# Other start addresses for the operands of the second MLP's matmuls, in a transform followed by two MLPs

## The chip, the cores and the metric

The kernel runs on one core of a Trainium2 chip, as one launch. The metric is the time of one execution in microseconds of device time; the kernel before takes 1510.42 us in the median of three runs (1510.21 to 1510.7). TensorE has two clock levels here, 1.2 and 2.4 GHz; the profile gives the granted clock as a share of the higher one.

## The reference

The input `x` has 4 batches of 3072 tokens with 256 features. A two-dimensional Fourier transform is taken over tokens and features and its real part kept. The result goes through an MLP and then through a second, gated one with a shift by one token:

```
x  = fft(fft(x, axis=1), axis=2).real                  # 12288 tokens, 256 features
h  = x @ w_in;  g = max(0.01 * h, h);  x = g @ w_out   # 256 -> 2048 -> 256
xk = mu_k * x + (1 - mu_k) * x_prev                    # x_prev: the token before
xr = mu_r * x + (1 - mu_r) * x_prev
k  = max(xk @ w_k, 0)                                  # 256 -> 1024
v  = (k * k) @ w_v                                     # 1024 -> 256
out = v / (1 + exp(-(xr @ w_r)))                       # gate, 256 -> 256
```

The weights come as 64-bit floats and are turned on the chip into pairs of 32-bit values.

## The kernel before

Precision is kept by pairs: each operand of a large matmul is held as a high and a low part in the type float32r, and a product is the sum of three matmuls, high by high, low weights by high, high weights by low. All large matmuls have 128 rows, 128 columns of weights and 512 moving columns. Moving and weight operands lie in SBUF; results go to PSUM.

The program has three stages in order of time. A set-up of some 120 us makes tables and the first weights. Then the transform and the first MLP run batch by batch in tiles of 512 tokens (until about 915 us). Last comes the second MLP in 24 tiles of 512 tokens (`for ti in range(len(tiles))`), which is the part that the change touches.

A tile of the second MLP is worked off in eight steps `f`, one for each 128 of the 1024 hidden features. In each step TensorE gets:

- six matmuls of `k_mm` (PSUM tile `kps`): the weights `kh`, `kl`, `kh` (called `wkh` and `wkl` in rows) against the mixed tokens `mh`, `mh`, `ml`, for two halves of the features each;
- in two of the eight steps six matmuls of `r_mm` (PSUM tile `rps`): `rh`, `rl`, `rh` against the high and low mix for the gate;
- six matmuls of `v_mm` (PSUM tile `v`) for a step that came two earlier: `vh`, `vl`, `vh` against the squared features `k2h`, `k2h`, `k2l`.

ScalarE and VectorE make in the meantime relu and square of a step (`k_ev`), its split in two parts (`k_split`) and the mix and split of the next tile (`prep`, one piece after each step). The lists `q1` and `q2` keep the squared features two steps ahead of `v_mm`. SP loads token tiles two ahead (`load_tile`) and stores results (`finish`). The engines follow this order as it is written; nothing reorders it.

Where a tile lies in SBUF is decided by pools: a pool puts the tags of its tiles one after the other in the order in which each tag is first asked for, a tag with several buffers taking several places. The six weights of the second MLP are the first tiles of the pool `w2p`, at the right end of SBUF, in the order kh, kl, vh, vl, rh, rl; everything else of this stage is in the pool `p2`. One small tile, `pad3`, begins `p2`. With it each of the six weight tiles and each tile of `p2` starts at 480 modulo 512 bytes of its partition. Slices within a tile start whole multiples of 512 bytes further on, so every moving operand and every weight block of these matmuls starts at 480 as well. There are two exceptions, both in the first tile of tokens: its mix (`prep_early`) and its first squared features lie in tiles of another pool, at 128 modulo 512. In the first MLP weights and moving operands start at 416, also alike.

Of the kernel before, what the change touches and what calls it, by code (L numbers as in the profile page):

```python
# [9 lines left out]
F32 = mybir.dt.float32  # L10
# [7 lines left out]
P = 128  # L18
# [29 lines left out]
def source(n):  # L48
    if n == 0:
        return D_, MID  # L50
    return (S_, place(n)) if n <= M else (D_, place(N - n))


def tile_tokens():
    at = {source(n): n for n in range(N)}
    return [[at[s, t * W + c] for c in range(W)] for s in (S_, D_) for t in range(NT)]


TOKENS = tile_tokens()


def runs_before(tokens):
    runs = []
    for c, n in enumerate(tokens):
        s, q = source(n - 1) if n else (None, 0)
        if runs and runs[-1][0] == s and s is not None and runs[-1][1] + runs[-1][3] == q:
            runs[-1][3] += 1
        else:
            runs.append([s, q, c, 1])
    return runs  # L70


def token_rows():
    rows = np.concatenate([np.array(t) for t in TOKENS])
    return np.concatenate([rows + b * N for b in range(B)])
# [3 lines left out]
def fft_mlp_kernel(ctx, tc, xa, xb, x7, x8, x87, tb, tbs, alt, ce, so, mu, w_in, w_out, w_k, w_v, w_r, out):  # L79
# [23 lines left out]
    def act_copy(o, i):  # L103
        A.activation(o, i, ACTF.Copy)  # L104
# [4 lines left out]
    def hi_lo(hi, lo, src):  # L109
        act_copy(hi, src)  # L110
        V.tensor_tensor(lo, src, hi.bitcast(F32), op=ALU.subtract)  # L111
# [556 lines left out]
    def w2_alloc():  # L668
        w2p = tc.alloc_tile_pool(name="w2p", bufs=1, side="right")
        w2["pool"] = w2p  # L670
        for nm, k, f in (("k", 2, FK), ("v", NK, D), ("r", 2, D)):
            for x in "hl":
                w2[nm + x] = w2p.tile([P, k, f], F32R, name=f"w{nm}{x}")
        w2["xp"] = tc.alloc_tile_pool(name="xp", bufs=1, side="right")
        for n in range(n_early):
            nm, _, at = sources[n]
            for x, k in zip("hl", kept[n]):
                Q.dma_start(at(w2[nm + x]).bitcast(F32), k)


    def w2_piece(n):
        z = {"fp": stage, "ft": "f"}
        nm, src, at = sources[n]

        def load():
            z["st"] = load_f64(src, 2, 256)

        def parts():
            if n < n_early:
                return (stage.tile([P, 2, 256], F32R, tag="r", bufs=3, name="wh"),  # L690
                        stage.tile([P, 2, 256], F32R, tag="h", bufs=2, name="wl"))
            return at(w2[nm + "h"]), at(w2[nm + "l"])

        one, two, three, four, five = split_steps(z, 2, 256, parts)

        def last():
            five()
            if n < n_early:
                for k, t in zip(kept[n], z["p"]):
                    Q.dma_start(k, t.bitcast(F32))  # L700
            if n + 1 < len(sources):
                w2_load[n + 1]()
        return load, [one, two, three, four, last]

    w2_load, w2_steps = [], []
    for n in range(len(sources)):
        a, c = w2_piece(n)
# [5 lines left out]
    def load_tile(ti):  # L713
# [5 lines left out]
        Q.dma_start(x, yd[b][s][:, :, t * W:(t + 1) * W])  # L719
        for s, q, c, n in runs_before(TOKENS[i]):  # L720
            if s is None:
# [5 lines left out]
    def prep(x, xprev, r):  # L727
        def mix(i, h, t, m):
            s = slice(2 * i + h, 2 * i + h + 1)
            A.activation(t[:, h], xprev[:, h], ACTF.Copy, scale=omu[:, s])  # L730
            V.scalar_tensor_tensor(m[:, h], x[:, h], mut[:, s], t[:, h], op0=ALU.mult, op1=ALU.add)

        def one(i, nm):
            z = {}

            def first():
                z["t"] = w2["p2"].tile([P, 2, W], F32, tag="mt", name="mt")
                z["m"] = w2["p2"].tile([P, 2, W], F32, tag="mx", name="mx")
                mix(i, 0, z["t"], z["m"])

            def split():
                hi = w2["p2"].tile([P, 2, W], F32R, tag=nm + "h", name="mh")
                lo = w2["p2"].tile([P, 2, W], F32R, tag=nm + "l", name="ml")
                hi_lo(hi, lo, z["m"])
                r[nm] = (hi, lo)
            return [first, lambda: mix(i, 1, z["t"], z["m"]), split]

        return one(0, "k") + one(1, "r")
# [34 lines left out]
    for b in range(B):  # L783
# [4 lines left out]
        for ti in range(NT):  # L788
# [3 lines left out]
            for u in range(NF):  # L792
                i = ti * NF + u
                x = nx
# [37 lines left out]
                if b == B - 1 and i == qe_u + 2:  # L832
                    fft.release()
                    w2_alloc()
# [79 lines left out]
    p2 = w2["p2"] = ctx.enter_context(tc.tile_pool(name="p2", bufs=2))  # L914
# [24 lines left out]
    def finish(ti, vps, sig):  # L939
# [5 lines left out]
        if ti < len(tiles) - 1:  # L945
            Q.dma_start(out[ti], o)

    def k_split(k2):
        hi = p2.tile([P, W], F32R, tag="k2h", bufs=3, name="k2h")
        lo = p2.tile([P, W], F32R, tag="k2l", bufs=3, name="k2l")  # L950
        hi_lo(hi, lo, k2)
        return hi, lo

# [13 lines left out]
    for ti in range(len(tiles)):  # L967
# [7 lines left out]
        for f in range(f0, NK):  # L975
            ps = ps2.tile([P, 512], F32, tag="k", bufs=2, name="kps")
            r = p2.tile([P, W], F32, tag="r", bufs=3, name="rl")
            k2 = p2.tile([P, W], F32, tag="k2", bufs=3, name="k2")
            k_mm(ps, f, rd["k"])
            k_ev(ps, r, k2)  # L980
            if q1:
                tt, ff, kk2 = q1.pop(0)
                q2.append((tt, ff, k_split(kk2)))
            q1.append((t, f, k2))
            t["rk"] = rd.get("r")
            if not end and g0 <= f < g0 + NB:
                gate(t, f - g0)
            if end and f == NK - 1:
                gate(t, 0)
            if len(q2) > 1:  # L990
                drain()
            if f == f0:
                for n in ((1, 2) if ti == 0 else (ti + 2,)):
                    if n < len(tiles):
                        loaded[n] = load_tile(n)
            if f == f1 and not end:
                for g in todo:
                    g()
                todo = do_prep(ti + 1)
            if todo:  # L1000
                todo.pop(0)()
    tt, ff, kk2 = q1.pop(0)
    q2.append((tt, ff, k_split(kk2)))
    gate(t, 1)
    drain()
# [79 lines left out]
```

## Time and profile before

| | |
|---|---|
| median of three runs | 1510.42 us |
| the profiled execution, its own time | 1511.04 us |
| its span, from the first instruction to the last | 1509.3 us |
| TensorE busy | 1479.3 us, 98% of the span |
| VectorE, ScalarE, GpSimd busy | 68%, 59%, 11% |
| second MLP, from 945 us to the end | 564 us, 2473 matmuls |
| granted clock of TensorE there | 1.00, which is 2.4 GHz |

A matmul's record overlaps the next one's: each lasts 0.39 us from its first read to its modelled last write, but the next starts after some 0.23 us. What a matmul costs is the distance from start to start. It is read best in groups: the chain of waits prints six consecutive matmuls of one kind as one piece, and the timeline gives the start of each group to 0.01 us.

### The profile page before, as it was taken

Reading aid. Unit: us, or ns where it says so; the run is one execution under the profiler, and the core shown is the slowest. Engines: PE = TensorE matmul, PEld = TensorE weight load, DVE = VectorE, ACT = ScalarE, POOL = GpSimd, SP = SyncE. Lnnn points to the kernel's source line nnn. Section 1 sums busy time; section 2 is a strip of 40 time slices with the busy share of each in tenths; the row PEclk is TensorE's granted clock in tenths of the full one; section 3 lists DMA queues with packets and bytes.
Section 4 is the critical chain, followed back from the end, with each engine's and each line's share of the span. In section 5 each row is a group of like instructions: output and inputs, shape, how many; then the busy total and the mean of one; then the engine's idle time right before and its main releaser. Section 6 shows DMA issues by size and latency. Waiting matters only on the chain.

```text
span 1509.3 us, 17754 instructions
## 1 busy us (share of the span) xinstructions
PE 1479.3 (98%) x6506; PEld 1212.3 (80%) x6506; DVE 1032.8 (68%) x1426; ACT 890.5 (59%) x1469; POOL 168.2 (11%) x165
## 2 busy tenths in 40 slices
PE   5899999999999999999999999999999999999998
PEld 3677888888888888888888887888888888888887
DVE  8776667676767766666667775766667676766665
ACT  2565566656566656566566665656555656565554
POOL 4333401023101142010001000000000000000000
PEclk8999999999999999999999999999999999999999
DMA  7434723276213464132411102221212121211200
GB/s 252 140 95 110 119 56 129 85 195 103 35 67 123 164 123 92 14 122 99 137 43 36 56 1 84 84 71 56 71 56 84 43 84 44 83 63 63 70 29 28
DMA packets 97810, 128.71 MB, mean 85 GB/s; under 512 B 29190, under 2 KB 64775, under 8 KB 94650
## 3 DMA queue, kind: packets, MB, share of 16 engines
q1 hardware_dynamic: 74618, 87.29, 18.0%
q0 software_dynamic: 23104, 40.29, 11.7%
q8 instruction: 51, 0.84, 0.2%
q14 instruction: 37, 0.30, 0.1%
HBM read 99.67 MB, written 27.88 MB: 85 GB/s over the span
## 4 chain that ended last, share of the span: by engine, by line
PE 95%; DVE 1%; DMA 1%; ACT 0%; issue 0%; POOL 0%; ACTq 0%; DVEq 0%
PE o L571 34%; PE v L927 17%; PE kps L884 17%; PE ps L560 9%; PE ps L548 9%; PE rps L935 4%; PE wps L383 1%; PE dps L592 0%; DMA pm<-in_xa 0%; DMA xl<-in_xb 0%; PE cps L434 0%; PE f0Qe L299 0%; PE f0Pe L299 0%; PE f1Qe L299 0%; PE f2Qe L299 0%; DMA y<-yo 0%
## 5 line engine op out<-in xcount | busy, mean ns | idle before, releaser
L637 DVE SCALAR_TENSOR_TENSOR g<-ev,ps 128x512 f32<-128x512 f32 x192 | 131.7, 686 | 194.5 <-PE ps L560 194.4
L888 ACT ACTIVATE rl<-kps 128x512 f32<-128x512 f32 x190 | 113.9, 599 | 230.4 <-PE kps L884 227.0
L619 DVE TENSOR_TENSOR gl<-g,gh 128x1024 fp32r<-128x1024 f32 x192 | 239.5, 1248 | 1.4 <-ACT gh L104 1.4
L889 DVE SCALAR_TENSOR_TENSOR k<-kps,rl 128x512 f32<-128x512 f32 x190 | 131.6, 693 | 148.4 <-ACT rl L888 147.7
L104 ACT ACTIVATE gh<-g 128x1024 fp32r<-128x1024 f32 x192 | 202.8, 1056 | 51.1 <-PE o L571 50.0
L107 ACT ACTIVATE g<-ps 128x512 f32<-128x512 f32 x192 | 114.9, 598 | 163.6 <-DVE g L637 162.2
L571 PE MATMUL o<-gh,uoh 128*128 128x512 f32 x768 | 211.3, 389 | 0.0
L571 PE MATMUL o<-gh,uol 128*128 128x512 f32 x768 | 211.1, 389 | 0.0
L571 PE MATMUL o<-gl,uoh 128*128 128x512 f32 x768 | 211.1, 389 | 0.0
L571 PEld LDWEIGHTS o<-gh,uoh 128*128 128x128 f32 x768 | 144.2, 188 | 30.4
L571 PEld LDWEIGHTS o<-gl,uoh 128*128 128x128 f32 x768 | 144.2, 188 | 30.0
L571 PEld LDWEIGHTS o<-gh,uol 128*128 128x128 f32 x768 | 144.2, 188 | 29.9
L553 DVE SCALAR_TENSOR_TENSOR ev<-cb,w,ps 128x512 f32<-128x512 f32 x192 | 143.4, 747 | 2.6 <-PE ps L548 0.8
L111 DVE TENSOR_TENSOR k2l<-k,k2h 128x512 fp32r<-128x512 f32 x190 | 129.6, 682 | 0.5 <-ACT k2h L104 0.5
L927 PE MATMUL v<-k2h,wvh 128*128 128x512 f32 x382 | 121.7, 389 | 0.1
L927 PE MATMUL v<-k2l,wvh 128*128 128x512 f32 x382 | 121.5, 389 | 0.0
L927 PE MATMUL v<-k2h,wvl 128*128 128x512 f32 x382 | 121.5, 389 | 0.0
L107 ACT ACTIVATE g<-g 128x512 f32<-128x512 f32 x192 | 119.6, 623 | 0.0
L884 PE MATMUL kps<-mh,wkh 128*128 128x512 f32 x380 | 117.3, 390 | 1.5 <-ACT mh L104 0.8
L104 ACT ACTIVATE k2h<-k 128x512 fp32r<-128x512 f32 x190 | 118.4, 623 | 0.0
L884 PE MATMUL kps<-ml,wkh 128*128 128x512 f32 x380 | 117.2, 390 | 0.1
L884 PE MATMUL kps<-mh,wkl 128*128 128x512 f32 x380 | 117.0, 389 | 0.0
(392 smaller groups left out, 2280.4 us busy)
## 6 DMA issues: line engine op xcount, KB each, us to landing
y<-yo SPq DMA_DIRECT2D x24, 512.0 KB
xa<-y SPq DMA_DIRECT2D x24, 512.0 KB
out_dram<-o SPq DMA_DIRECT2D x23, 512.0 KB
tab_c<-in_tbs POOLq DMA_DIRECT2D x6, 1158.0 KB, 5.8
tab_d<-in_tbs POOLq DMA_DIRECT2D x6, 1158.0 KB, 5.5
tab_a<-in_tbs POOLq DMA_DIRECT2D x6, 1158.0 KB, 6.2
tab_b<-in_tbs POOLq DMA_DIRECT2D x6, 1158.0 KB, 5.5
xl<-in_xa SPq DMA_DIRECT2D x24, 256.0 KB
```

Of the source, the lines that this page charges most:

```text
L104: A.activation(o, i, ACTF.Copy)
L107: A.activation(o, i, ACTF.Prelu, alpha=0.01)
L111: V.tensor_tensor(lo, src, hi.bitcast(F32), op=ALU.subtract)
L548: T.matmul(x["ps"], l[:, f], r, start=(i == 0), stop=(i == 2))
L553: V.scalar_tensor_tensor(x["ev"], x["cb"], w128[:, u:u + 1], x["ps"], op0=ALU.mult, op1=ALU.add)
L560: T.matmul(x["ps"], l[:, f], r, start=False, stop=(i == 2), skip_group_check=True)
L571: T.matmul(po[s][h], w[:, u % HF, h * P:(h + 1) * P], g[:, s], start=(u == 0 and i == 0), stop=(u == NF - 1 and i == 2))
L619: V.tensor_tensor(gl, x["g"], x["gh"].bitcast(F32), op=ALU.subtract)
L637: V.scalar_tensor_tensor(g[:, 1], x["ev"], 2.0, x["ps"], op0=ALU.mult, op1=ALU.subtract)
L884: T.matmul(ps, w[:, k, sl], x[:, k], start=(i == 0), stop=(i == 5))
L889: V.scalar_tensor_tensor(k2, ps, 0.0, r, op0=ALU.max, op1=ALU.mult)
L927: T.matmul(vps[m], w[:, f, m * P:(m + 1) * P], x, start=(f == 0 and i == 0), stop=(f == NK - 1 and i == 2))
```

## The change

Nothing is added to or taken from what the engines execute. On all five engines the same instructions stand in the same order with the same waits and the same semaphore values; only the numbers in the tiles' names shift, since there are new tiles. These are nine gaps, tiles that nobody reads or writes. Six stand in `w2p`, one behind each weight tile, and move the weights and what follows in that pool. Three stand in `p2`: 32 bytes ahead of `k2h`, 480 behind `k2l` and 32 ahead of the gate's mix; the set `gaps` lets each be made once.

```
+GAPS = {"kh": 128, "kl": 160, "vh": 256, "vl": 64, "rh": 32, "rl": 128}
...
                 w2[nm + x] = w2p.tile([P, k, f], F32R, name=f"w{nm}{x}")
+                w2p.tile([P, GAPS[nm + x] // 4], F32, name=f"gap{nm}{x}")
...
             def split():
+                if nm == "r":
+                    gap("c", 32)
                 hi = w2["p2"].tile([P, 2, W], F32R, tag=nm + "h", name="mh")
...
+    gaps = set()
+
+    def gap(k, n):
+        if k not in gaps:
+            gaps.add(k)
+            p2.tile([P, n // 4], F32, tag="gap" + k, bufs=1, name="gap" + k)
+
     def k_split(k2):
+        gap("a", 32)
         hi = p2.tile([P, W], F32R, tag="k2h", bufs=3, name="k2h")
         lo = p2.tile([P, W], F32R, tag="k2l", bufs=3, name="k2l")
+        gap("b", 480)
```

Where the operands start, modulo 512 bytes, as the two built programs place them:

| operand | before | after |
|---|---|---|
| kh, kl | 480, 480 | 224, 352 |
| vh, vl | 480, 480 | 0, 256 |
| rh, rl | 480, 480 | 320, 352 |
| `mh`, `ml` for k_mm (tiles 1 to 23) | 480 | 0 |
| `mh`, `ml` for r_mm (all tiles) | 480 | 0 |
| `k2h`, `k2l` | 480 | 0 |
| first tile's mix and first squared features | 128 | 128 |
| tiles that only ScalarE, VectorE and DMAs use (`r`, `k2`, `sig`, `xa`, `xb`, `mt`, `mx`) | 480 | 480 |
| `o`, the result tile | 480 | 0 |

## Rows read from the trace of the kernel before

**Rows 1.** Page: busy time, clock slices, and the chain by line.
```profile
PE 1479.3 (98%) x6506; PEld 1212.3 (80%) x6506; DVE 1032.8 (68%) x1426; ACT 890.5 (59%) x1469; POOL 168.2 (11%) x165
...
PEclk8999999999999999999999999999999999999999
...
PE o L571 34%; PE v L927 17%; PE kps L884 17%; PE ps L560 9%; PE ps L548 9%; PE rps L935 4%; PE wps L383 1%; PE dps L592 0%; DMA pm<-in_xa 0%; DMA xl<-in_xb 0%; PE cps L434 0%; PE f0Qe L299 0%; PE f0Pe L299 0%; PE f1Qe L299 0%; PE f2Qe L299 0%; DMA y<-yo 0%
```
**Rows 2.** Busy time by stretch: stretch, length, busy time (instructions) of each engine, clock, DMA.
```profile
945.00:1509.00 564.00, 560.44 (x2473) 463.74 (x2471) 380.92 (x553) 328.53 (x545) 0.00 (x0) 1.00 0.19 62
1000.00:1500.00 500.00, 500.00 (x2207) 414.01 (x2207) 338.13 (x491) 292.83 (x486) 0.00 (x0) 1.00 0.18 60
```
**Rows 3.** Groups of TensorE: count, busy, mean ns of one, idle before (page, and whole run).
```profile
L927 PE MATMUL v<-k2h,wvh 128*128 128x512 f32 x382 | 121.7, 389 | 0.1
L884 PE MATMUL kps<-mh,wkh 128*128 128x512 f32 x380 | 117.3, 390 | 1.5 <-ACT mh L104 0.8
...
L935 PE MATMUL rps<-mh,wrh 128*128 128x512 f32 x96 | 29.6, 389 | 0.0
```
**Rows 4.** Chain of waits, settled second MLP: start, length, what, matmuls.
```profile
1101.52 1.36 PE kps L884 x6
1102.88 1.36 PE rps L935 x6
1104.24 1.36 PE v L927 x6
```
**Rows 5.** Chain of waits, first tiles of the second MLP.
```profile
927.08 1.40 PE kps L884 x6
928.48 1.39 PE rps L935 x6
929.87 1.39 PE v L927 x6
931.25 1.40 PE kps L884 x6
...
942.40 1.36 PE kps L884 x6
```
**Rows 6.** Timeline of TensorE, transform matmuls of 384 columns and what follows them.
```profile
234.30 0.52 PE L299 MATMUL f1Po<-tab_c,sh1Po 128*128 128x384 f32 x2
234.66 0.33 PE L299 MATMUL f1Po<-tab_c,sl1Po 128*128 128x384 f32 x1
234.83 0.51 PE L299 MATMUL f1Po<-tab_c,sh1Po 128*128 128x384 f32 x2
...
235.89 0.40 PE L560 MATMUL ps<-Qh,wh 128*128 128x512 f32 x1
236.12 0.40 PE L560 MATMUL ps<-Ql,wh 128*128 128x512 f32 x1
236.36 0.39 PE L560 MATMUL ps<-Qh,wl 128*128 128x512 f32 x1
236.58 0.39 PE L548 MATMUL ps<-Ph,wh 128*128 128x512 f32 x1
236.81 0.40 PE L548 MATMUL ps<-Pl,wh 128*128 128x512 f32 x1
237.05 0.39 PE L548 MATMUL ps<-Ph,wl 128*128 128x512 f32 x1
237.28 1.08 PE L571 MATMUL o<-gh,uoh 128*128 128x512 f32 x4
```
**Rows 7.** Timeline of TensorE, matmuls in plain float32 (two records for each).
```profile
65.38 2.11 PE L299 MATMUL f0Pe<-tab_a,pm 128*128 128x386 f32 x6
67.33 0.81 PE L306 MATMUL f0Pe<-altt,e7p 128*128 128x386 f32 x2
```
**Rows 8.** Who waited for whom, 950 us to the end: total, times, longest.
```profile
ACT rl L888 <- PE kps L884: 219.0, 180, 1.9
DVE k L889 <- ACT rl L888: 137.4, 156, 1.7
```

## The prediction

> **What bounds the kernel now.** I read the page first. TensorE is busy for 98% of the span, its clock stands at the full level in every slice behind the first, and the chain that ended last lies on its lines almost throughout; 38% of the span is the three lines of the second MLP, 17, 17 and 4 [rows 1]. Then the busy time by stretch: from 1000 to 1500 us TensorE is busy for 500.00 of 500 us, while VectorE works 338 and ScalarE 293 [rows 2]. Then the waits: ScalarE's relu waits 219 us for `kps`, and VectorE's square waits for that relu [rows 8]. So in this stage everybody waits for TensorE and TensorE for nobody. What its matmuls cost from start to start is the time of the stage.
>
> That cost is not simply the number of columns. At 2.4 GHz 512 columns take 213.3 ns. In the settled stage six matmuls take 1.36 us, be they k, r or v [rows 4], which is 226.7 ns for one; 2207 matmuls in 500 us say the same, 226.6 [rows 2]. So 13.3 ns come on top of each. Where I looked next is whether this extra is fixed, because if it is, start addresses can't matter.
>
> It is not fixed. In the first tiles the same code with the same shapes takes 1.39 to 1.40 us for six, 231.7 to 233.3 ns each, and from 942 us on 1.36 [rows 5]. No engine is waited for between these pieces. What differs in the first tile is the place of the operands: its k matmuls have moving operands at 128 modulo 512 and weights at 480, so the weights stand 352 ahead; later both stand at 480. The v and r groups between them have equal starts, yet they too take 1.39. The extra therefore depends on the pair of starts and on what ran just before. The same is seen behind a transform group in the first MLP: steps of 0.23, 0.24, 0.22, 0.23, 0.24 and 0.23 us with equal starts, together 1.39 (from 235.89 to 237.28) [rows 6], before it falls back to the even step. A stream with equal starts finds an even step of 226.7; disturbed, it walks through longer and shorter ones first.
>
> **The change part by part.** Removed, added or moved instructions: none, and no wait changes. The gaps cost SBUF space and nothing else.
>
> How many steps change: the moving operand goes from 480 to 0, and its weights to their six new places, in 380 x 3 matmuls of k less the 36 of the first tile, in 382 x 3 of v, and in 96 x 3 of r [rows 3]: 1104 + 1146 + 288 = 2538. They take 2538 x 226.7 ns = 575 us now. Of their offsets between weights and moving operand, vh keeps equal starts (0 and 0); kh gets 224, kl and rl 352, vl 256, rh 320.
>
> The trace shows none of these mixtures settled, so I bound the step from both sides.
> - From above: the disturbed first tiles, 1.40 us for six [rows 5], 233.3 ns, which is 6.7 more than now. For all 2538 that is +16.9 us.
> - In between: the transform's nine matmuls of 384 columns, whose moving operands start at 352 to 392 and whose weights start at 480, go from 234.30 to 235.89 [rows 6]: 1.59 us, 176.7 each, 16.7 above their 160.0 ns of columns. As 512 columns with that extra, 230.0 ns: +8.5 us. Single ones among them are cheaper: 0.17 us (234.66 to 234.83), 10 above the columns.
> - From below: plain float32, which takes its columns at half the pace. Six records of 386 columns go from 65.38 to 67.33 [rows 7], 325 ns each against 321.7 for the columns, so 3.3 above. Most of the extra thus belongs to reading at full pace, and a stream that never stumbles would take 213.3 + 3.3 = 216.7 ns, 10.0 less than now: -25.4 us.
>
> I take 223.3 ns, the columns and an extra of 10.0, for two reasons that I rate and can't prove. First, 10 above the columns is the shortest step that unequal starts show for 384 columns, and a step of 0.22 us is in the trace for 512 (236.36 to 236.58) [rows 6]; both are read to 0.01 us, so this value has 10 ns of play. Second, those short steps come singly because with one offset for all matmuls a short step is followed by one that starts late and is long. With different offsets within a group, the following matmul meets another offset, and a repeating pattern of twelve or eighteen matmuls can settle where short steps follow each other. Against 226.7 that is 3.3 ns less, 2538 x 3.3 = 8.5 us.
>
> The other parts together are small. In the first tile 54 matmuls (36 and 12 of k, 6 of v) keep their moving operand at 128 and get other weights; at 10 ns each way that is 0.5 us at most, and I take nothing. ScalarE and VectorE write `k2h`, `k2l`, `mh` and `ml` at other places and SP stores `o` from one. If all their work there got a tenth longer, VectorE would come to 372 of 500 us, still far under TensorE, so TensorE covers it; without that cover the tenth would cost 34 us in 500. If TensorE's step shortens, what is late next is again the square of the step, but it is used two steps later and VectorE has 32% of the stretch idle [rows 2], so no wait takes the place of the 3.3 ns.
>
> Sum, against the profiled execution: 1511.04 - 8.5 = 1502.5 us. That execution lies 0.6 above the median of the runs, so 1501.9 for the median.
>
> A rule of the Trainium skill speaks against all this. The trace: same shapes, same engine, no wait in the chain, 1.40 us for six in one place and 1.36 in another [rows 5]. The page "SBUF — State Buffer", section "Who interferes with whom", gives TensorE two independent read ports, one for moving operands and one for weights, and says that it never waits on anyone; the page "TensorE: Matmul & The Clock Gate", section "Back-to-back issue gap", puts the isolated step at columns over clock plus about 2.5 ns, an estimate of 215.8 ns for 512. By the ports alone no address would matter and the sum would be 1510.4; the trace does not agree, since neither 226.7 nor a difference of 6.7 follows from it.
>
> **The rivals.**
> - The stream never settles. Place: every k, r and v group. kl and rl get just the offset, 352, that the first tile has, and there neither the groups at 352 nor the equal ones between them got under 1.39 in tens of groups. Against it: the first tile has six matmuls of one offset in a row. It decides from a mean step over 226.7, so six over 1.36. At the full price +16.9 us, 1527.3; with the transform's extra of 16.7, +8.5, 1518.9. Slower than before. Between the two, nearer the second, since vh keeps equal starts.
> - No change: the pattern settles on an even 226.7 again, because what fixes the even step is not the offset but the pace of the moving stream. For it: k, r and v, the first MLP with 416 and the second with 480 all have the very same even step. Against it: rows 5. 1510.4. The page "SBUF — State Buffer" of the Trainium skill, section "Who interferes with whom", ends at this time too.
> - The extra goes nearly to that of plain float32: 216.7, -25.4 us, 1485.0. For it: moving operands now begin on a multiple of 512, so each row of 2048 bytes covers whole blocks. Against it: the first tile's operands at 128 are whole multiples of smaller blocks, and it was slow.
>
> **How the numbers follow.** The forecast (steps between some 218 and 225 ns, 1490 to 1507) gets 0.47; the floor 0.08; no change 0.15; the stream that doesn't settle 0.30, which is high because the only long sample of an unequal offset is a slow one. Faster by over 0.2% (3.0 us, about what this measurement can tell from no change) is the first two, 0.55; within 0.2%, 0.15; slower, 0.30. The range runs from 1490, under which about one in twelve is left, to 1521, which takes in the middle price of the slow case and leaves about one in nine above. The likeliest case by itself is 1490 to 1507.
>
> **What would show it.** The chain's pieces of six in the second MLP: 1.34 for the forecast, 1.36 for no change, 1.38 to 1.40 for the slow case, 1.30 for the floor. They should be unlike for k, v and r now, as the offsets are. More than 2473 matmuls should fit into 564 us, 2511 by the forecast. In the first MLP nothing should move. If TensorE shows waits for ScalarE or VectorE in that stage, or if the first tiles alone change, the account by steps is wrong; a mean step above 226.7 makes the prediction wrong in sign.

## The result and the profile after

The changed kernel takes 1523.35 us in the median of four runs (1521.1 to 1523.66), the kernel before 1510.43; the ratio is 1.0082, 95% interval 1.0065 to 1.01. It is 12.9 us slower, where 8.5 us faster was forecast, and 2.35 us above the upper end of the range. The first rival, a step above 226.7 ns (given 0.30), is what happened.

Page after, span, busy time and the clock slices:

```profile
span 1519.3 us, 17754 instructions
...
PE 1490.0 (98%) x6506; PEld 1209.5 (80%) x6506; DVE 1032.1 (68%) x1426; ACT 890.9 (59%) x1469; POOL 169.3 (11%) x165
...
PEclk8999999999999999999999999999999999999999
```

Busy time by stretch, after (stretch, length, busy time and instructions of each engine, clock, DMA):

```profile
945.00:1509.00 564.00, 564.00 (x2436) 456.56 (x2435) 375.04 (x544) 325.12 (x539) 0.00 (x0) 1.00 0.18 61
1000.00:1500.00 500.00, 500.00 (x2159) 404.77 (x2158) 332.68 (x481) 288.62 (x478) 0.00 (x0) 1.00 0.18 59
```

TensorE has no idle time in 1000 to 1500 us and the full clock, as before [rows 2]. But 2159 matmuls fit there where 2207 did: 500 us over 2159 is 231.6 ns for a step, 5.0 more than 226.6. For the 2538 changed matmuls that is 12.7 us, the whole difference within the spread of the runs. Who waits for whom is as before too [rows 8]: ScalarE's wait for `kps` grows by 10.4 us and VectorE's wait for the relu by 9.8, and TensorE waits for nobody.

```profile
ACT rl L892 <- PE kps L888: 229.4, 180, 1.9
DVE k L893 <- ACT rl L892: 147.2, 157, 1.8
```

The chain of waits after, in the settled stage (start, length, what, matmuls):

```profile
1099.82 1.40 PE rps L939 x6
1101.22 1.38 PE v L931 x6
1102.60 1.39 PE kps L888 x6
1103.99 1.40 PE rps L939 x6
1105.39 1.38 PE v L931 x6
1106.77 1.40 PE kps L888 x6
```

Before, all three kinds took 1.36 [rows 4]. Now k and r take 1.39 to 1.40, and v, whose offsets are 0 and 256, 1.38. In nanoseconds between the starts of consecutive matmuls, as the trace has them, v goes 236, 224, 231, 236, 228, 229 and k 236, 232, 228, 231, 236, 233, with a nanosecond or so of play, time after time: 184 pieces of v have a sum of 1384 or 1385, 182 of k one of 1395 or 1396.

One number has to be read with care. The profiled execution took 1521.1 us, 2.25 less than the median, since its set-up, whose instructions are the same, ended earlier. The first MLP's matmul `dps` shows it, in the kernel before and in the changed one:

```profile
350.04 0.40 PE L592 MATMUL dps<-wh,dcs 128*2 128x512 f32 x1
```

```profile
347.64 0.40 PE L593 MATMUL dps<-wh,dcs 128*2 128x512 f32 x1
```

TensorE's clock bears on it. From 49 to 53 us of the set-up the granted clock was 0.50 (1.2 GHz) in the profile before and 1.00 (2.4 GHz) in the one after, and 18 matmuls fell into these 4 us instead of 11 (before, then after; columns as above):

```profile
49.00:53.00 4.00, 3.74 (x11) 3.19 (x12) 2.75 (x5) 1.28 (x4) 0.00 (x0) 0.50 1.02 403
```

```profile
49.00:53.00 4.00, 3.07 (x18) 2.68 (x17) 3.29 (x5) 1.31 (x4) 0.00 (x0) 1.00 1.02 411
```

From `dps` on the two run alike to the end of the first MLP; the second MLP alone, from its first matmul to the last, is 12.5 us longer.

### The profile page after: what moved, and what is told of

It is laid out like the page before. It is cut to its first block, busy times and chain, and to the rows that moved or that the text cites. A ratio compares the mean times of both kernels' runs of the same rounds, so it can differ in the third digit from the quotient of the medians.

```text
span 1519.3 us, 17754 instructions
## 1 busy us (share of the span) xinstructions
PE 1490.0 (98%) x6506; PEld 1209.5 (80%) x6506; DVE 1032.1 (68%) x1426; ACT 890.9 (59%) x1469; POOL 169.3 (11%) x165
## 4 chain that ended last, share of the span: by engine, by line
PE 95%; DVE 1%; DMA 1%; ACT 0%; issue 0%; POOL 0%; ACTq 0%; DVEq 0%
PE o L572 34%; PE v L931 17%; PE kps L888 17%; PE ps L561 9%; PE ps L549 9%; PE rps L939 4%; PE wps L384 1%; PE dps L593 0%; DMA pm<-in_xa 0%; PE cps L435 0%; DMA xl<-in_xb 0%; PE f0Qe L300 0%; PE f0Pe L300 0%; PE f1Qe L300 0%; PE f2Qe L300 0%; DMA y<-yo 0%
```

## The experiments

Three theories. A: the step hangs on the offset between weights and moving operand. B: the new place of the moving operands costs. C: the new places of the weights cost. Each edit is against the changed kernel; a gap of 0 makes no tile.

**All equal at 0.**

```
-GAPS = {"kh": 128, "kl": 160, "vh": 256, "vl": 64, "rh": 32, "rl": 128}
+GAPS = {"kh": 0, "kl": 0, "vh": 0, "vl": 0, "rh": 0, "rl": 480}
```

> The moving operands stay at 0 modulo 512 as in the changed kernel, and all six weight tiles are put at 0 too. Theory A (the step hangs on the offset between weights and moving operand; equal starts give the even 226.7 ns): pieces of six at 1.36 us in k, r and v, time 1510 to 1511. Theory B (the new start of the moving operands by itself costs): pieces of 1.38 to 1.40 as in the changed kernel, 1521 to 1524. Theory C (the weights' own places cost, wherever the moving operands are): v's vh was at 0 already, so v stays at 1.384 and k and r go to about the same, 1520 to 1522.

1510.28 us, ratio to the kernel before 0.9997 (0.9988 to 1.0007). Its chain:

```profile
1101.77 1.36 PE kps L889 x6
1103.13 1.36 PE rps L940 x6
1104.49 1.36 PE v L932 x6
```

B has fallen: the moving operands stand where the changed kernel has them, and nothing is lost.

**The moving operands alone** (weights all at 480).

```
-GAPS = {"kh": 128, "kl": 160, "vh": 256, "vl": 64, "rh": 32, "rl": 128}
+GAPS = {"kh": 0, "kl": 0, "vh": 0, "vl": 0, "rh": 0, "rl": 0}
```

> Moving operands at 0, all six weight tiles left at 480: one offset, 480, for everything. A: not even, pieces of six between 1.38 and 1.40, time 1517 to 1528, with k, r and v alike, since their offset is the same. B: as the changed kernel, 1521 to 1524. C: as the kernel before, 1.36 and 1510.

1526.06 us, ratio 1.0104 (1.0087 to 1.0121). C has fallen, since the weights stand where they always stood:

```profile
1100.78 1.40 PE v L932 x6
1102.18 1.40 PE kps L889 x6
1103.58 1.40 PE rps L940 x6
```

**The weights alone** (moving operands at 480).

```
-        gap("a", 32)
+        gap("a", 0)
...
-        gap("b", 480)
+        gap("b", 0)
...
-                    gap("c", 32)
+                    gap("c", 0)
```

> Weights at 224, 352, 0, 256, 320 and 352 as in the changed kernel, moving operands left at 480: offsets 256, 384, 32, 288, 352, 384. A: not even, 1.38 to 1.40 for six and 1517 to 1528, with other single steps than in the changed kernel. B: 1.36 and 1510. C: as the changed kernel, 1521 to 1524, with the same single steps.

1524.1 us, ratio 1.0095 (1.008 to 1.011), with other single steps than the changed kernel: most often 229, 235, 232, 235, 231, 236 for v. So each half alone costs at least as much as both together (15.5 and 13.5 us above the kernel before on the same chip), though the new moving starts cost nothing with weights at 0 and the old weights cost nothing with moving operands at 480. What counts is how the two stand to each other: A stands.

**A sweep of offsets.** To measure the step by itself, a kernel of nothing but matmuls, each row of 48 at one pair of starts (`wl` equals `wh` here, `REPEAT` is 8). This sweep and the three that follow are one execution each, read in the stretch where the granted clock is 1.00. Its core:

```
for m, wh, wl in plan():
    for _ in range(REPEAT):
        acc = ps.tile([P, W], F32, tag="s", name="acc")
        for i, (w, k) in enumerate([(wh, 0), (wh, 1), (wl, 0), (wl, 1), (wh, 0), (wh, 1)]):
            a, c = w // 4 + (n % 8) * P, m // 4 + k * W
            T.matmul(acc, wt[:, a:a + P], mv[:, c:c + W], start=(i == 0), stop=(i == 5))
            n += 1
```

> No transform and no MLP: after one load it runs rows of 48 matmuls (128x128 weights, 512 moving columns, float32r, groups of six into two PSUM tiles), each row at one pair of starts: moving at 0, 128 and 480 with weights at every multiple of 32, moving at 0 with weights at odd multiples of 16, moving at 16 with weights at multiples of 64; then all rows again in reverse order. No other engine works meanwhile. A: the settled step is a function of the offset alone, 226.7 ns at offset 0 for every start of the moving operand, and at others 223 to 234; what the row before was does not matter. B: one value for each start of the moving operand, over all weights. C: one value for each start of the weights. A fourth, D (other engines' traffic makes the long steps): 226.7 or less everywhere, since nothing else runs.

Two neighbouring rows of 48 matmuls with moving operands at 0, weights at 256 and then at 288, as stretches from a row's first start to the next row's first:

```profile
99.76:110.64 10.88, 10.88 (x49) 9.01 (x48) 0.00 (x0) 0.00 (x0) 1.00 0.00 0
110.64:121.84 11.20, 11.20 (x50) 9.02 (x49) 0.00 (x0) 0.00 (x0) 1.00 0.01 1
```

The columns are TensorE, its loading of weights, ScalarE and GpSimd; VectorE has no instruction here. 48 starts lie in each stretch (the counts take in neighbours that reach over the edge): 226.7 ns and 233.3 ns a step. The other engines do nothing, so D has fallen: no other engine's traffic is needed for a long step. The means over the settled half of each row agree for moving operands at 0, 128 and 480, and for weights 256 bytes apart, within the spread that the table gives. By offset, weights less moving operand, modulo 256:

| offset | ns a step | offset | ns a step |
|---|---|---|---|
| 0 | 226.7 | 128 | 232.3 to 233.5 |
| 16 | 233.3 | 144 | 233.4 |
| 32 | 233.3 to 233.4 | 160 | 233.1 to 233.4 |
| 48 | 233.3 | 176 | 230.0 |
| 64 | 233.2 to 233.4 | 192 | 228.7 to 229.0 |
| 80 | 232.0 to 232.1 | 208 | 231.7 to 232.0 |
| 96 | 234.1 to 234.6 | 224 | 233.3 to 233.5 |
| 112 | 233.3 | 240 | 228.4, once 226.7 |

So A holds with a period of 256, not 512, but not as strictly as it was put. With the moving operand at 16 instead of 0, 128 or 480 the table shifts: offset 240 takes 231.5 to 231.8, and offset 48 takes 230.0 in one order of the rows and 234.5 in the other. Offsets 16 and 240 have two settled steps as well: in other sweeps, and for 240 once in this one, they came to 226.7. So the row that ran before does matter for some layouts. And the entry counts: in the longest case of eleven, a row with equal starts behind one with offset 16, the first steps are 233, 231, 233, 236, 224, 231, 236, 228, 233 and 231 before 226 and 227 are reached. From 236 on the first five are the first five of v in the changed kernel, but v has only six steps, and then k breaks the series again.

That made two theories for v: A1, its own offset of 256 costs; A2, offset 256 is as good as 0 and v only inherits the disturbed start from k and r.

**k and r equal, v as changed.**

```
+GAPS = {"kh": 0, "kl": 0, "vh": 256, "vl": 256, "rh": 0, "rl": 480}
```

> The changed kernel with k's and r's four weight tiles put back to equal starts (0, moving operands at 0); v as in the changed kernel, vh at 0 and vl at 256. Theory A2 (only the offset modulo 256 counts, and v is long in the changed kernel because k and r hand it a disturbed start): 1.36 for k, r and v alike, 1510 to 1511. Theory A1 (v's own offset of 256 costs): v stays near 1.384, k and r 1.36 to 1.37, 191 groups of v give some 4.6 us: 1514 to 1516.

1510.24 us, ratio 1.0004 (0.9994 to 1.0013):

```profile
1101.36 1.36 PE kps L889 x6
1102.72 1.36 PE rps L940 x6
1104.08 1.36 PE v L932 x6
```

**v equal, k and r as changed.**

```
+GAPS = {"kh": 128, "kl": 160, "vh": 0, "vl": 320, "rh": 32, "rl": 128}
```

> The other half: vl is put to 0 as vh is, k's and r's weights stay at 224, 352, 320 and 352. A2: nothing changes against the changed kernel, v 1.384 in the same single steps although all its starts are equal, k 1.396, time 1522 to 1524. A1: v comes to 1.36, 1517 to 1519.

1522.28 us, ratio 1.0081 (1.0066 to 1.0096), and v in the same steps as in the changed kernel although all its starts are equal:

```profile
1104.52 1.40 PE rps L940 x6
1105.92 1.38 PE v L932 x6
1107.30 1.40 PE kps L889 x6
```

A2 stands: the whole loss comes from the four tiles of k and r, and over a third of it is paid in v's matmuls (1146 steps of 230.7 against 226.7, 4.6 us of 12.7).

**A sweep of pairs**, moving operands at 0, 256 pairs (h, l):

```
...
-    return one + one[::-1]
+    return [(0, h, l) for h in range(0, 256, 16) for l in range(0, 256, 16)]
```

> As the sweep of offsets, no MLP, moving at 0, rows of 48 matmuls in groups of six with a high and a low weight start (h, h, l, l, h, h), both at every multiple of 16 under 256. If the even step of 226.7 ns is a floor, no pair gets under it and only pairs of 0 with 0 (or of starts close to 256) reach it. If mixtures can be cheaper, as the prediction had it, some pairs settle at 220 to 225. The pair of the changed kernel's k (224, 96) should give 232 to 234, and mixtures should lie between their two offsets' values of the first sweep.

The least of 256 rows is 226.7; the mean is 231.8. Fourteen pairs reach the least, all of them of starts 0, 16, 144 and 240. Changing offsets within a group never gives less, which refutes the reason that the prediction rated and could not prove. What a mixture can do is to undercut its dearer half: 144 by itself takes 233.4, with 0 or 240 it takes 226.7. Two details of the expectation missed: mixtures don't lie between their two values (192 with 0 takes 230.4), and the pair of the changed kernel's k, 224 and 96, takes 231.5 here, against 232.7 for k in the kernel, where v and r stand in between.

**A sweep of shapes**, one start for all weights of a row:

```
T.matmul(acc[:cols, :width], wt[:, a:a + cols], mv[:, c:c + width], start=(i == 0), stop=(i == 5))
```

> As the sweep of offsets, no MLP, moving at 0, weights at every multiple of 16 under 256, with other shapes: 64, 32 and 2 columns of weights instead of 128, then 384 and 256 moving columns with 128 of weights. Theory W (the reading of the next weights collides with the moving stream): with fewer columns of weights the difference between offsets shrinks, and at 2 columns every offset takes the same, at most 226.7; with fewer moving columns the extra in ns stays. Theory S (each matmul waits for a start slot that its two starts decide): the differences between offsets stay as they are with 2 columns.

Both theories missed a part. With 2 columns of weights the differences between offsets are nearly gone, as W said: 231.7 ns at 14 of 16 offsets, 231.1 at one. But it is 231.7, not 226.7 or less; only offset 16 gives 226.7. And with 64 and 32 columns the differences don't shrink on the way there, but fall on other offsets: 226.7 (at 144) to 235.5 and 228.9 to 240.0, with 230.0 and 231.7 at equal starts. The busy time of the rows with 128, 64, 32 and 2 columns shows how little the amount of weights matters:

```profile
20.00:180.00 160.00, 160.00 (x691) 129.58 (x690) 0.00 (x0) 0.00 (x0) 1.00 0.00 1
190.00:350.00 160.00, 160.00 (x696) 93.25 (x695) 0.00 (x0) 0.00 (x0) 1.00 0.00 1
360.00:530.00 170.00, 170.00 (x734) 79.99 (x733) 0.00 (x0) 0.00 (x0) 1.00 0.00 0
550.00:710.00 160.00, 160.00 (x694) 57.95 (x693) 0.00 (x0) 0.00 (x0) 1.00 0.00 1
```

The loading of weights (second busy time) falls from 129.58 to 57.95 us, the number of matmuls in 160 us stays at 691 to 696 (the third stretch is 170 us long). So the reading of weights shapes the pattern, and with 128 columns and equal starts the step is even the least, but the length of the reading is not the extra itself. Whether a matmul that loads no weights would have the extra, no run shows. With 384 moving columns 10 of 16 offsets take 173.3, with 256 the least is 113.3 and the most 120.0, which is what equal starts take there.

**A sweep of moving starts**, alternating or walking on from matmul to matmul:

```
rows = [([0, x], [w]) for x in range(16, 256, 16) for w in range(0, 256, 32)]
for d in range(16, 256, 16):
    walk = [i * d % 256 for i in range(16)]
    rows += [(walk, [0]), (walk, walk)]
```

> As the sweeps before, no MLP, rows of 72 matmuls. First the moving start alternates between 0 and x (every multiple of 16 under 256) with weights at every multiple of 32 under 256; then it walks on by a fixed amount from matmul to matmul, with the weights at 0 or walking along. [...]

The question was whether any order of moving starts gets under 226.7. The least of 150 rows is again 226.7 (starts alternating between 0 and 64, weights at 64), the mean of the alternating ones 231.7, and walking along gives 228.3 at best. In none of the 478 rows of 512 columns and 128 of weights (72 pairs of starts, 256 pairs of weights, 150 moving orders) is there a layout under the kernel before, so no faster version was built.

**Does the map hold in the kernel?** All weights at 192, and then a mixture of 0 and 256 in every group:

```
+GAPS = {"kh": 0, "kl": 0, "vh": 0, "vl": 0, "rh": 0, "rl": 288}
```

> The changed kernel with all six weights at 192, moving operands at 0. If the map of the sweeps holds in the kernel, a step settles at 228.8 to 229.0 in k, r and v alike, pieces of six at 1.37 to 1.38, and 2538 x 2.2 ns = 5.6 us on top of the kernel before: 1515 to 1517. If a mixed neighbourhood (other engines reading and writing the same memory) sets the step, it goes to 231 to 233 as in the changed kernel: 1521 to 1527.

1516.28 us, ratio 1.0036 (1.0023 to 1.0049), as the table says:

```profile
1100.45 1.37 PE rps L940 x6
1101.83 1.37 PE v L932 x6
1103.20 1.37 PE kps L889 x6
```

```
+GAPS = {"kh": 256, "kl": 0, "vh": 256, "vl": 256, "rh": 256, "rl": 224}
```

> kh and rl at 256, kl and rh at 0, vh at 0 and vl at 256, moving operands at 0: each group mixes offsets 0 and 256. Modulo 256 rule: 1.36 everywhere, 1510 to 1511. Modulo 512 rule: k and r mixed and not even, 1.38 to 1.40, 1517 or more.

1510.67 us, ratio 0.9998 (0.9989 to 1.0008), 1.36 in all three kinds:

```profile
1100.88 1.36 PE kps L889 x6
1102.24 1.36 PE rps L940 x6
1103.60 1.36 PE v L932 x6
```

## Why the prediction was wrong

- **What bounds the kernel**: right. TensorE's steps are the stage's time, nothing else moved, and 2538 times the change of the step is the difference of the runs.
- **The extra depends on the pair of starts and on what ran before**: right, shown by the first three experiments and the first sweep. The Trainium skill's page "SBUF — State Buffer", section "Who interferes with whom", by which TensorE never waits on anyone, does not account for it: with all other engines idle, the step still went from 226.7 to 233.3 ns by the place of the weights alone.
- **The step that failed** is the second reason for 223.3 ns: "a repeating pattern of twelve or eighteen matmuls can settle where short steps follow each other". The pattern of twelve does settle and repeats to the nanosecond, but at 2.780 us against 2.720. A step of 224 is in it, in v, and it follows one of 236. No pair of the sweep settles under 226.7. Short steps do stay in a settled pattern, but long ones stay beside them and weigh more.
- **The value** was taken from the shortest single steps of [rows 6], read to 0.01 us, while the sums of the same rows, 176.7 ns for 384 columns and 231.7 for six of 512, stood beside them. In nanoseconds the two single steps are 172 and 224, which is 12.0 and 10.7 above their columns, not 10. As an estimate of a mean, the mean of the rows was the better guide: their in-between price gave 1518.9 and the dearest 1527.3, and 1523.35 lies between. The six steps of 512 columns there are 233, 236, 224, 231, 236 and 228: from 236 on, the first five steps of v in the changed kernel. So most of v's settled round stood in the trace before, with its long steps beside the short one.
- **The offsets were read modulo 512.** vl at 256 counted as an unlike start; it is a like one. kl and rl at 352 are 96 modulo 256, the dearest entry of the table. That v nevertheless became dear is the carry-over from k and r.
- **The first rival** had price and place right, every k, r and v group, though the time lies midway between its two prices and not nearer 1518.9. Its mechanism was half right: the stream does settle, on a dear pattern. Its reason, the first tiles at 352, was the right evidence, if overstated: the chain there shows some ten groups, not tens, and one of them, with equal starts, is under 1.39:

```profile
934.05 1.37 PE v L927 x6
```

- **Late next, and the small parts**: nothing came; ScalarE's and VectorE's new places changed no wait of TensorE.

## What to carry to other kernels

Where float32r matmuls of 512 moving columns and 128 columns of weights follow each other without a gap, compare the distance from start to start with the columns over the clock, and place weights and moving operands at equal starts modulo 256 bytes. For other shapes take a sweep first: with 64 columns of weights, or 256 moving columns, equal starts were not the cheapest. A disturbed start took up to ten steps to settle here, so one unlike operand in a series also makes its like neighbours dear. An unsettled sample in a trace (a first tile, a short group between others) gives its mean as evidence for unlike starts, not its shortest step. A sweep of 72 pairs of starts, two rows of 48 matmuls each, in one launch settled what three edited kernels could only rank.

## What was not expected of the hardware

- The settled sums followed here, over one round of their pattern, are whole multiples of 6.67 ns, 16 columns at 2.4 GHz, though single steps such as 224 or 231 are not: 226.7 is 34 of them, 233.3 is 35, v and k together (2.780 us) are 417, 384 columns take 26 (173.3) and 256 columns 17 at least (113.3). The even step of 512 columns is two above the columns' 32. What beats there, and why the period in the address is 256 bytes, no run shows.
- Fewer columns of weights don't get under 226.7: at 2 columns the step is 231.7 at nearly every offset, 5 ns longer than with 128 at equal starts.
- Two settled steps exist for one layout: offset 16 took 233.3 in one sweep and 226.7 in two others, and with the moving operand at 16 offset 48 took 230.0 in one order of the rows and 234.5 in the other. Only what ran before differs.
